# Reordering the attention steps on each engine, and a convolution accumulator and feature sums that use PSUM

## The chip, the core and the metric

One core of a Trainium2 chip runs the whole program. Its engines are TensorE (matmuls; PE in the profile, with the weight loads in a row of their own, PEld), VectorE (DVE), ScalarE (ACT), GpSimd (POOL) and SyncE (SP), which here only issues DMAs. Each engine takes its instructions in the order in which they were written into its queue; semaphores hold one back until what it needs is done. The metric is the device time of one execution in microseconds (us), the median of three runs.

## The reference, cut to what matters

Three stages follow each other on 8 batches of 576 positions (8 heads of 64):

```python
def _attn_ref(q, k, v, w_phi):            # linear attention
    def phi(x):
        proj = x @ w_phi                  # 64 -> 128
        proj = proj - max(abs(proj), axis=-1)
        return concat([exp(proj), exp(-proj)])
    kv = phi(k).T @ v ; z = sum(phi(k))
    return (phi(q) @ kv) / (phi(q) @ z + 1e-6)

def _moe_ref(x, w_val, conv_w, w_out):    # the mixing, d_model 512
    gate = sigmoid(causal_conv(x, conv_w))            # 5 taps per channel
    return (gate * (x @ w_val)) @ w_out

def _moe2_ref(x, w_ch1, w_ch2):           # Fourier mixing, norm, MLP
    u = x + real(fft(fft(x, axis=1), axis=2))
    un = (u - mean) / sqrt(var + 1e-6)
    return u + relu(un @ w_ch1) @ w_ch2
```

The weights of the last two stages arrive as 64-bit floats.

## The kernel before

**Attention.** A pair of batches and a pair of heads make a unit; there are 16 units, each cut into 5 groups of position chunks (four groups of two chunks and one of a single chunk), so TOT = 80 pieces. `run_attention` is a loop over steps `st`, written in a manual schedule: the order of the calls in a step is the order on every engine. A piece passes through these calls, each some steps after the first:

- `emit_P` (step 0): TensorE projects keys and queries into the PSUM tile `pj` (two buffers).
- `emit_Y` (1): VectorE takes the maximum (L210) and subtracts it (L211) into `y`, which frees `pj`.
- `emit_kE` (1): ScalarE, two exponentials of the key half (L219, L220).
- `emit_KV` (2): TensorE, keys by values into `kv`; `emit_kvT` (2): VectorE copies `kv` out (L253).
- `emit_yT` (2): TensorE transposes the query half of `y` into a `tr` buffer (L261), and ScalarE takes two exponentials out of it, `qe` (L263, L264). There are two `tr` buffers, used in turn by `emit_yT` and `emit_XT`.
- `emit_num` (5): TensorE, queries by `kv` into `nm` (one buffer, L279); `emit_X` (5): VectorE divides (L288 to L290), which frees `nm`; `emit_XT` (6): TensorE transposes the quotient (L303), ScalarE copies it to `xT` (L307), SP stores it to `x_scr`.

Between these the weights are converted from 64 bits: 21 generators (`convert`), each resumed at four steps (`lead`): a load from SP, then VectorE L94 and ScalarE L95, then L97, L98 and GpSimd L99 and L100, then ScalarE L102 (the sign) and GpSimd L103 and L104. For the first four of them `done` adds a ScalarE copy (L66) that needs the result of L104. Steps 72 on load the first two batches of the mixing (`load_x`, into the two buffers which the raw weights used too).

**Mixing.** `emit_taps` makes the convolution of one channel block in an SBUF tile `acc` (two buffers): ScalarE writes the first tap (L412), VectorE adds four (L414, scalar_tensor_tensor, read and written in place). `emit_V` takes its sigmoid (L426), multiplies it into the product `val` from PSUM (L434), and makes sums (`gs`) and their high and low parts (`ge`, ScalarE and GpSimd). `emit_W` multiplies by w_out into PSUM tiles `x2p`, copies them out on ScalarE (L457) and, for c of 2 and 3, makes the sums and differences `fs` of two SBUF operands on VectorE (L462), whose high and low parts `fh` feed the transform along features (`emit_FD`, tiles `yp`); `emit_SD` does the one along positions (`abp`). `x2p`, `yp` and `abp` take turns in one PSUM pool of six banks; `val` has two. `split_x` makes the high and low parts `xh` of the next batch on ScalarE and GpSimd. The order here is not written out: the framework's list scheduler sets it from a timing model of its own. The convolutions of the first two blocks (batch 0, m of 0 and 1) are issued in the attention's last steps, each as a whole, in steps 78 and 80, and `emit_V(0, m)` in steps 81 to 84.

**The rest.** The last batch pair (`run_last`) and the MLP (`run_mlp`) are ordered by a planner (`place_ops`) and are not touched but for the pool that two of six PSUM tiles of `run_last` come from.

## Time and profile before

| | us |
|---|---|
| median of three runs | 1487.26 |
| the three runs | 1485.99 to 1487.38 |
| the profiled execution | 1487.67 |
| its span, first to last instruction | 1485.9 |
| TensorE busy | 1358.8 |
| VectorE busy | 1286.4 |
| ScalarE busy | 813.6 |
| GpSimd busy | 743.5 |

The time outside the span is 1.8 us. Times in the trace count from the start of the span. The attention loop takes the first 340 us, its last steps and the first products of the mixing reach to about 395, the mixing to about 655, `run_last` to about 730, the MLP to the end.

### The profile page before, as it was taken

Reading aid. Unit: us, or ns where it says so; the run is one execution under the profiler, and the core shown is the slowest. Engines: PE = TensorE matmul, PEld = TensorE weight load, DVE = VectorE, ACT = ScalarE, POOL = GpSimd, SP = SyncE. Lnnn points to the kernel's source line nnn. Section 1 sums busy time; section 2 is a strip of 40 time slices with the busy share of each in tenths; the row PEclk is TensorE's granted clock in tenths of the full one; section 3 lists DMA queues with packets and bytes.
Section 4 is the critical chain, followed back from the end, with each engine's and each line's share of the span. In section 5 each row is a group of like instructions: output and inputs, shape, how many; then the busy total and the mean of one; then the engine's idle time right before and its main releaser. Section 6 shows DMA issues by size and latency. Waiting matters only on the chain.

```text
span 1485.9 us, 35178 instructions
## 1 busy us (share of the span) xinstructions
PE 1358.8 (91%) x14672; PEld 1305.0 (88%) x14672; DVE 1286.4 (87%) x1938; ACT 813.6 (55%) x1513; POOL 743.5 (50%) x526
## 2 busy tenths in 40 slices
PE   5899999898799999996889999999999999999998
PEld 5788888787788898896789999999999999999998
DVE  5688888877999999989899999999989878887776
ACT  4777787764444444454645555555556544454442
POOL 3847777732577878846455655555526111111111
PEclk8899999999899999997899999999999999999999
DMA  6347766661133333233542223232233222222211
GB/s 218 134 157 269 256 236 245 237 226 40 63 121 128 135 135 104 96 131 126 173 139 92 89 77 114 86 114 94 90 119 105 85 83 86 86 86 86 79 43 51
DMA packets 89852, 186.99 MB, mean 126 GB/s; under 512 B 10455, under 2 KB 37335, under 8 KB 87518
## 3 DMA queue, kind: packets, MB, share of 16 engines
q1 hardware_dynamic: 88488, 181.33, 35.8%
q10 hardware_dynamic: 1206, 3.41, 0.6%
q8 instruction: 115, 1.88, 0.5%
q14 instruction: 43, 0.35, 0.1%
HBM read 121.79 MB, written 62.93 MB: 124 GB/s over the span
## 4 chain that ended last, share of the span: by engine, by line
PE 36%; DVE 28%; POOL 13%; issue 8%; ACT 7%; DMA 6%; SPq 0%; DVEq 0%; POOLq 0%; ACTq 0%
PE cx L857 9%; PE x L788 9%; PE cy L857 5%; PE y L788 4%; DVE acc L414 3%; DVE A L629 3%; DMA raw<-in_w_ch_dram 3%; DVE c L629 3%; PE z L788 3%; DVE acc L629 2%; PE cz L857 2%; POOL ge L75 2%; DVE s L733 2%; POOL mt L100 2%; POOL xh L75 2%
## 5 line engine op out<-in xcount | busy, mean ns | idle before, releaser
L857 PE MATMUL cx<-h,w 128*128 128x256 f32 x1152 | 175.4, 285 | 4.8 <-ACT h L66 2.5
L857 PEld LDWEIGHTS cx<-h,w 128*128 128x128 f32 x1152 | 157.5, 193 | 6.7 <-ACT h L66 3.1
L414 DVE SCALAR_TENSOR_TENSOR acc<-xf,cw,acc 128x576 f32<-128x576 f32 x128 | 137.4, 1078 | 9.1 <-ACT acc L412 7.5
L629 POOL TENSOR_TENSOR c<-c,c 128x512 f32<-128x512 f32 x35 | 49.8, 1424 | 167.6 <-ACT h L632 127.9
L66 ACT ACTIVATE h<-c 128x512 fp32r<-128x512 f32 x180 | 111.7, 627 | 39.8 <-DVE c L629 22.4
L629 DVE TENSOR_TENSOR acc<-cx,acc 128x512 f32<-128x512 f32 x144 | 98.1, 681 | 33.8 <-PE cx L857 33.0
L788 PE MATMUL x<-un,w 128*128 128x256 f32 x864 | 117.2, 286 | 6.7 <-DVE eo L629 6.0
L75 POOL TENSOR_TENSOR h<-c,h 128x512 fp32r<-128x512 f32 x33 | 48.3, 1465 | 149.6 <-ACT h L66 149.3
L632 ACT ACTIVATE c<-c 128x512 f32<-128x512 f32 x108 | 67.9, 630 | 99.8 <-DVE c L629 98.5
L857 PE MATMUL cy<-h,w 128*128 128x256 f32 x864 | 117.3, 285 | 5.2 <-ACT un L66 2.3
L788 PEld LDWEIGHTS x<-un,w 128*128 128x128 f32 x864 | 109.9, 193 | 7.6 <-issue 6.2
L857 PEld LDWEIGHTS cy<-h,w 128*128 128x128 f32 x864 | 108.9, 192 | 7.7 <-DVE h L72 2.5
L72 DVE TENSOR_TENSOR h<-c,h 128x512 fp32r<-128x512 f32 x111 | 104.4, 941 | 1.2 <-ACT h L66 0.5
L240 PE MATMUL kv<-vraw,ke 128*64 128x66 f32 x2560 | 97.5, 231 | 8.4 <-DVE kvT L253 4.9
L203 PE MATMUL pj<-wp,kqraw 64*128 64x128 f32 x1152 | 91.7, 298 | 14.4 <-DMA kqraw<-in_k_dram 7.1
L240 PEld LDWEIGHTS kv<-vraw,ke 128*64 128x64 f32 x2560 | 85.6, 143 | 19.4 <-DVE kvT L253 5.1
L203 PEld LDWEIGHTS pj<-wp,kqraw 64*128 64x128 f32 x1152 | 75.5, 198 | 29.3 <-issue 13.1
L99 POOL TENSOR_SCALAR mt<-mt 128x1024 f32<-128x1024 f32 (+1 forms) x21 | 55.7, 2650 | 88.3 <-DVE r L288 52.7
L211 DVE TENSOR_TENSOR y<-pj,m 128x1024 f32<-128x1024 f32 (+1 forms) x80 | 89.5, 1118 | 8.7 <-ACT xT L307 0.5
L210 DVE TENSOR_REDUCE m<-pj 128x8 f32<-128x1024 f32 (+1 forms) x80 | 88.6, 1108 | 5.5 <-PE pj L203 5.5
L75 POOL TENSOR_TENSOR ge<-gs,ge 128x580 fp32r<-128x580 f32 x32 | 53.6, 1675 | 76.8 <-ACT ge L66 76.8
L79 PE MATMUL val<-xh,wv 128*128 128x288 f32 x256 | 77.3, 307 | 11.2 <-DVE gv L434 11.2
(249 smaller groups left out, 4284.2 us busy)
## 6 DMA issues: line engine op xcount, KB each, us to landing
raw<-in_w_ch_dram SPq DMA_DIRECT2D x16, 1024.0 KB, 7.4
wr<-w_scr SPq DMA_DIRECT2D x32, 448.0 KB, 3.6
vraw<-in_v_dram SPq DMA_DIRECT2D x16, 660.0 KB, 7.7
x_scr<-xT SPq DMA_DIRECT2D x32, 288.0 KB, 5.1
xf<-x_scr SPq DMA_DIRECT2D x8, 1152.0 KB, 5.9
out_dram<-acc SPq DMA_DIRECT2D x36, 256.0 KB, 2.2
kqraw<-in_k_dram SPq DMA_DIRECT2D x15, 576.0 KB, 6.8
kqraw<-in_q_dram SPq DMA_DIRECT2D x15, 576.0 KB, 7.0
```

The source lines that it names most:

```text
L66: nc.scalar.activation(out=dst, in_=src, func=ACTF.Copy)
L72: nc.vector.tensor_tensor(out=dst, in0=src, in1=f32(hi), op=ALU.subtract)
L75: nc.gpsimd.tensor_tensor(out=dst, in0=src, in1=f32(hi), op=ALU.subtract)
L79: mm(o, ah, bh, start=first, stop=False)
L203: mm(p[:, h, o:o + F], t[r, w, 128 * c:128 * c + 128], wp[r, :], start=True, stop=True)
L210: nc.vector.tensor_reduce(out=m, in_=pv, axis=AX.X, op=ALU.max, apply_absolute_value=True)
L211: nc.vector.tensor_tensor(out=y, in0=pv, in1=m.unsqueeze(3).to_broadcast([128, 2, 2 * n, F]), op=ALU.subtract)
L240: mm(t[p, w, :], e[:, a, h, j, p], tv[:, h, slot, :], start=slot % 5 == 0 and w == 0, stop=slot % 5 == 4 and w == 3, skip_group_check=True)
L414: nc.vector.scalar_tensor_tensor(out=acc, in0=x[:, m, t:t + S], scalar=cw[:, m, t:t + 1], in1=acc, op0=ALU.mult, op1=ALU.add)
L629: op(e, cols, lambda e: (nc.vector if e == "v" else nc.gpsimd).tensor_tensor(out=o, in0=x, in1=y, op=alu), r, w)
L788: mm(p[:, n], l, v[:, kt], start=first and n + kt + m == 0, stop=kt == 1 and m == 2, skip_group_check=True)
L857: mm(p[:, o], v, r[:, n], start=first and o + n + m == 0, stop=n + m == 3, skip_group_check=True)
```

## The change

In `run_attention`, a step now issues `emit_X`, `emit_yT` and `emit_XT` first (each of X and XT one step later than before, so that their place behind the previous step's calls is the same), then `emit_P`, `emit_Y`, the weight pieces, `emit_kE`, `emit_KV`, `emit_kvT`, and `emit_num` last. The last resumption of a weight piece comes two steps after the third instead of one. The pools of `e` and `y` lose a buffer each; `xs` gains one. The convolutions of the first two blocks are split over steps 73 to 80, one VectorE tap each, and `emit_V(0, m)` is issued in steps 81, 82, 84 and 86.

In the mixing, from block 2 of batch 0 on, `acc` is a PSUM tile (one buffer, two banks, half of the positions in each), which ScalarE writes and VectorE updates there; the sigmoid goes from it to an SBUF tile `sg`. The sums `fs` take one operand straight from the PSUM tile of the product, each as soon as its product is there. The common pool of PSUM banks shrinks from six to four; `run_last` gets its other two from a pool that is opened when the mixing's are closed.

```diff
--- before.py
+++ after.py
@@ -150,15 +150,16 @@
     P["xf"] = pool(gx, "xf", 2, side=R)
     P["xh"] = pool(gx, "xh", 1, side=R)
     P["g"] = pool(gx, "g", 2, side=R)
-    e_p = pool(early, "e", 4, side=R)
-    y_p = pool(early, "y", 3, side=R)
+    e_p = pool(early, "e", 3, side=R)
+    y_p = pool(early, "y", 2, side=R)
     stg = pool(early, "stg", 2, side=R)
     vraw_p = pool(early, "vraw", 2, side=R)
     ps_pj = pool(early, "ps_pj", 2, PSUM, side=R)
     ap1 = pool(att, "ap1", 1)
     qe_p = pool(att, "qe", 4)
     sm_p = pool(att, "sm", 2)
-    xs_p = pool(att, "xs", 2)
+    xs_p = pool(att, "xs", 3)
+    xT_p = pool(att, "xT", 2)
     ps_tr = pool(att, "ps_tr", 2, PSUM)
     ps_kv = pool(att, "ps_kv", 1, PSUM)
     ps_nm = pool(att, "ps_nm", 1, PSUM)
@@ -302,7 +303,7 @@
         for j in range(n):
             nc.tensor.transpose(t[:, j, :], x[:, j].rearrange("p h d -> p (h d)"), ident)
         if g == 0:
-            xT[u] = xs_p.tile([128, 2 * S], F32, tag="xT", name="xT")
+            xT[u] = xT_p.tile([128, 2 * S], F32, tag="xT", name="xT")
         o = xT[u][:, 128 * cs[0]:128 * (cs[0] + n)]
         nc.scalar.activation(out=o, in_=t.rearrange("p c s -> p (c s)"), func=ACTF.Copy)
         if g == NG - 1:
@@ -368,11 +369,12 @@
         P["g0"] = pool(gx, "g0", 1, side=R)
         P["ws"] = pool(vx, "ws", 2, side=R)
         P["psv"] = pool(vx, "psv", 2, PSUM, side=R)
+        P["psa"] = pool(vx, "psa", 1, PSUM, side=R)
 
     def open_mix2():
         P["x2"] = pool(mx, "x2", 1)
         P["fs"] = pool(mx, "fs", 1)
-        P["ps"] = pool(mx, "ps", 6, PSUM)
+        P["ps"] = pool(mx, "ps", 4, PSUM)
         one = pool(mx, "one", 1)
         P["xr"] = [one.tile([128, NE], F32R, name=f"xr{i}") for i in range(2)]
         P["rem"] = [one.tile([128, NL], F32R, name=f"rem{a}") for a in range(2)]
@@ -406,15 +408,27 @@
 
     taps = {}
 
-    def emit_taps(b, m):
+    def tap_steps(b, m):
         x = xf[b]
-        acc = P["g"].tile([128, S], F32, tag="acc", name="acc")
-        nc.scalar.activation(out=acc, in_=x[:, m, 4:4 + S], func=ACTF.Copy, scale=cw[:, m, 4:5])
+        if "psa" in P:
+            acc = P["psa"].tile([128, 2, 512], F32, tag="pa", name="acc")[:, :, 0:HS]
+        else:
+            acc = P["g"].tile([128, 2, HS], F32, tag="acc", name="acc")
+
+        def shifted(t):
+            return x[:, m, t:t + S].rearrange("p (a s) -> p a s", a=2)
+        nc.scalar.activation(out=acc, in_=shifted(4), func=ACTF.Copy, scale=cw[:, m, 4:5])
         for t in range(4):
             nc.vector.scalar_tensor_tensor(
-                out=acc, in0=x[:, m, t:t + S], scalar=cw[:, m, t:t + 1], in1=acc, op0=ALU.mult, op1=ALU.add
+                out=acc, in0=shifted(t), scalar=cw[:, m, t:t + 1], in1=acc, op0=ALU.mult, op1=ALU.add
             )
+            if t < 3:
+                yield
         taps[b, m] = acc
+        yield
+
+    def emit_taps(b, m):
+        drain(tap_steps(b, m))
 
     def emit_V(b, m):
         h, l = xhl[b]
@@ -422,8 +436,9 @@
             geo[b] = tuple(P[f"g{b % 2}"].tile([128, 4, 2, NE], F32R, tag=f"g{i}", name="ge") for i in range(2))
         if (b, m) not in taps:
             emit_taps(b, m)
-        acc = taps.pop((b, m))
-        nc.scalar.activation(out=acc, in_=acc, func=ACTF.Sigmoid)
+        t = taps.pop((b, m))
+        acc = P["g"].tile([128, S], F32, tag="sg", name="sg")
+        nc.scalar.activation(out=acc.rearrange("p (a s) -> p a s", a=2), in_=t, func=ACTF.Sigmoid)
         gv = P["g"].tile([128, S + 2], F32, tag="gv", name="gv")
         for n in range(2):
             p = P["psv"].tile([128, HS], F32, tag="ps", name="val")
@@ -455,11 +470,12 @@
                 ws = slice(c * 128, (c + 1) * 128)
                 mm3(p, (wo[0][:, kk, ws], wo[1][:, kk, ws]), (gh[:, kk, a], gl[:, kk, a]), kk == 0, kk == 3)
             nc.scalar.activation(out=t[:, c, a, :], in_=p, func=ACTF.Copy)
+            if c >= 2:
+                if a == 0:
+                    fs = P["fs"].tile([128, 2, NE], F32, tag="fs", name="fs")
+                nc.vector.tensor_tensor(out=fs[:, a], in0=t[:, c - 2, a], in1=p, op=(ALU.add, ALU.subtract)[a])
         if c >= 2:
             c0 = c - 2
-            fs = P["fs"].tile([128, 2, NE], F32, tag="fs", name="fs")
-            for a, op in ((0, ALU.add), (1, ALU.subtract)):
-                nc.vector.tensor_tensor(out=fs[:, a], in0=t[:, c0, a], in1=t[:, c, a], op=op)
             fh, fl = fhl[b]
             hi_act(fh[:, c0], fs)
             lo_dve(fl[:, c0], fs, fh[:, c0])
@@ -981,7 +997,8 @@
             o_act(u[0:1, 2], w[96:97], ACTF.Copy, S, wk + [("u", 0, 0), ("u", 0, 1)], [("u", 0, 0), ("u", 0, 1)])
         o_dma([(u_scr[b].rearrange("c p s -> p c s"), u)], [("u", i, j) for i in range(2) for j in range(2)], [("u_scr", b)], 1152, K["su"])
     def run_last(b):
-        ps = [P["ps"].tile([128, 512], F32, tag="ps", name=f"ps{i}") for i in range(6)]
+        ps = [P["ps"].tile([128, 512], F32, tag="ps", name=f"ps{i}") for i in range(4)]
+        ps += [P["ps2"].tile([128, 512], F32, tag="ps2", name=f"ps{i}") for i in (4, 5)]
         ring = ((("ps", i % 6), ps[i % 6]) for i in range(1000))
         tl["fs"] = P["fs"].tile([128, 2, NE], F32, tag="fs", name="fs")
         tl["eo"] = P["x2"].tile([128, 2, 4, NE], F32, tag="eo", name="eo")
@@ -1140,39 +1157,43 @@
 
 
     def run_attention():
-        lead = (0, 3, 4, 5)
+        lead = (0, 3, 4, 6)
         todo = {}
+        tap0 = chain(tap_steps(0, 0), tap_steps(0, 1))
+        taps_at = range(X_AT + 1, X_AT + 9)
         for i in range(len(pieces)):
             for l in lead:
                 todo.setdefault(i * (X_AT - 2 - lead[-1]) // (len(pieces) - 1) + l, []).append(pieces[i])
         n_t = 2 * len(tables)
         did_t = 0
         with tc.manual_schedule():
-            for st in range(TOT + 7):
+            for st in range(TOT + 8):
                 u, g = divmod(st, NG)
 
                 def at(lag):
                     return 0 <= st - lag < TOT
 
+                if at(6):
+                    emit_X(st - 6)
+                if at(2):
+                    emit_yT(st - 2)
+                if at(7):
+                    emit_XT(st - 7)
                 if at(0):
                     emit_P(st)
                 if at(1):
                     emit_Y(st - 1)
+                for c in todo.get(st, ()):
+                    next(c)
+                if at(1):
                     emit_kE(st - 1)
                 if at(2):
                     emit_KV(st - 2)
+                    emit_kvT(st - 2)
+                if st in taps_at:
+                    next(tap0)
                 if at(5):
                     emit_num(st - 5)
-                if at(2):
-                    emit_kvT(st - 2)
-                for c in todo.get(st, ()):
-                    next(c)
-                if at(2):
-                    emit_yT(st - 2)
-                if at(5):
-                    emit_X(st - 5)
-                if at(6):
-                    emit_XT(st - 6)
                 if g == 1 and u >= 1 and u + 1 < NU:
                     load_kq(u + 1)
                 if g == 2 and u >= 1 and u + 1 < NU:
@@ -1186,13 +1207,11 @@
                     load_x(1)
                 if 0 <= st - X_AT - 2 < 4:
                     split_x(0, (st - X_AT - 2,))
-                if st in (TOT - 2, TOT):
-                    emit_taps(0, (st - TOT + 2) // 2)
                 if st == TOT + 1:
                     early.close()
                     open_mix()
-                if 1 <= st - TOT < 5:
-                    emit_V(0, st - TOT - 1)
+                if st - TOT in (1, 2, 4, 6):
+                    emit_V(0, (1, 2, 4, 6).index(st - TOT))
 
 
     if True:
@@ -1228,6 +1247,7 @@
             vx.close()
             gx.close()
             P["x2b"] = pool(mx, "x2b", 1)
+            P["ps2"] = pool(mx, "ps2", 2, PSUM)
             open_mlp()
             run_last(b)
             break
```

## Rows read from the trace of the kernel before

**Rows 1.** The page: busy time and share of the span of each engine.

```profile
PE 1358.8 (91%) x14672; PEld 1305.0 (88%) x14672; DVE 1286.4 (87%) x1938; ACT 813.6 (55%) x1513; POOL 743.5 (50%) x526
```

**Rows 2.** Busy time of each engine in four stretches (us from the span's start): length, then PE, PEld, DVE, ACT and POOL busy, the granted TensorE clock, the DMA engines' share and GB/s.

```profile
20.00:340.00 320.00, 284.86 (x6009) 253.14 (x6007) 257.94 (x446) 239.49 (x456) 216.72 (x94) 0.98 0.60 211
340.00:395.00 55.00, 38.38 (x456) 36.40 (x453) 44.21 (x76) 23.87 (x44) 15.27 (x15) 0.81 0.16 54
395.00:655.00 260.00, 239.85 (x1746) 233.22 (x1745) 247.90 (x382) 119.18 (x264) 197.71 (x192) 0.98 0.33 114
730.00:1486.00 756.00, 726.02 (x5963) 716.99 (x5962) 663.76 (x930) 383.67 (x661) 277.93 (x202) 1.00 0.28 90
```

**Rows 3.** Who waited for whom in the attention loop (0 to 345 us): total us, times, longest.

```profile
PE yt L261 <- ACT qe L264: 16.8, 13, 4.4
...
ACT cv L102 <- POOL mt L100: 16.1, 16, 1.9
...
ACT wv L66 <- POOL mt L104: 7.0, 2, 4.0
...
PE xt L303 <- ACT qe L264: 5.5, 1, 5.5
```

**Rows 4.** Timeline (start, us, engine, line, operation) of ScalarE, GpSimd and TensorE at the end of one of the first four weight pieces; in brackets the idle time before and what ended it.

```profile
59.52 1.16 ACT L102 ACTIVATE cv<-raw 128x1024 f32<-128x1024 int32 x1
63.87 1.06 ACT L66 ACTIVATE wo<-mt 128x1024 fp32r<-128x1024 f32 x1 [3.19 <-POOL mt L104]
...
61.50 2.34 POOL L104 TENSOR_TENSOR mt<-mt,cv 128x1024 f32<-128x1024 f32 x1
...
65.95 1.10 PE L261 MATMUL yt<-ident,y 128*128 128x128 f32 x4 [4.35 <-ACT qe L264]
```

**Rows 5.** Timeline of VectorE and TensorE: the end of `emit_Y` against the start of the transposes `yt` of the piece before, in the first and the last of 20 steps (of 73 looked at, steps 7 to 79) in which the transposes started first.

```profile
73.62 1.23 DVE L211 TENSOR_TENSOR y<-pj,m 128x1024 f32<-128x1024 f32 x1
...
74.77 0.44 PE L261 MATMUL yt<-ident,y 128*128 128x128 f32 x2
...
334.15 1.23 DVE L211 TENSOR_TENSOR y<-pj,m 128x1024 f32<-128x1024 f32 x1
...
334.97 0.66 PE L261 MATMUL yt<-ident,y 128*128 128x128 f32 x4
```

**Rows 6.** Timeline of VectorE, SP and ScalarE around the load of the mixing's first two batches (step 72) and its first use.

```profile
316.55 0.07 DVE L395 MEMSET xf<- 128x16 f32 x1
...
319.62 0.16 DVE L288 TENSOR_SCALAR r<-nm 128x4 f32<-128x4 f32 x1 [1.66 <-PE nm L279]
...
318.71 0.95 SPq L396 DMA_DIRECT2D xf<-x_scr  x2
...
328.29 0.68 ACT L66 ACTIVATE xh<-xf 128x576 fp32r<-128x576 f32 x1 [3.38 <-DMA xf<-x_scr]
```

**Rows 7.** Timeline of VectorE, TensorE and ScalarE between the attention and the mixing.

```profile
341.58 3.38 DVE L414 SCALAR_TENSOR_TENSOR acc<-xf,cw,acc 128x576 f32<-128x576 f32 x4 [1.75 <-ACT acc L412]
...
347.75 2.91 PE L240 MATMUL kv<-vraw,ke 128*64 128x66 f32 x48 [4.87 <-DVE kvT L253]
...
375.25 10.84 DVE L414 SCALAR_TENSOR_TENSOR acc<-xf,cw,acc 128x576 f32<-128x576 f32 x8 [0.94 <-ACT acc L412]
...
384.23 0.68 ACT L426 ACTIVATE acc<-acc 128x576 f32<-128x576 f32 x1 [4.49 <-DVE acc L414]
...
386.52 0.61 PE L79 MATMUL val<-xh,wv 128*128 128x288 f32 x1 [9.06 <-DVE gv L434]
```

**Rows 8.** What TensorE waited for in the mixing (395 to 655 us): total us, times, longest.

```profile
PE yp L79 <- ACT fh L66: 10.7, 6, 2.6
PE val L80 <- POOL xh L75: 8.2, 14, 2.7
```

**Rows 9.** Busy time in one iteration of the mixing loop, columns as in rows 2.

```profile
457.66:496.65 38.99, 35.47 (x262) 34.37 (x262) 37.75 (x59) 18.14 (x41) 31.28 (x30) 1.00 0.37 129
```

**Rows 10.** Durations of the operations that the change touches or is priced by. The first two and the last rows are groups (busy us, mean ns | idle before); in the others a number like 790/870/1903 is least/median/most ns. First four iterations (435 to 592 us), then three of them, the whole mixing, and the MLP.

```profile
L414 DVE SCALAR_TENSOR_TENSOR acc<-xf,cw,acc 128x576 f32<-128x576 f32 x64 | 68.5, 1071 | 2.2 <-ACT acc L412 1.5
...
L462 DVE TENSOR_TENSOR fs<-x 128x290 f32<-128x290 f32 x16 | 18.2, 1136 | 0.0
...
L414 DVE SCALAR_TENSOR_TENSOR acc<-xf,cw,acc x48: 790/870/1903, 460.6 to 573.0; 128x576 f32<-128x576 f32 x48
...
L434 DVE TENSOR_TENSOR gv<-val,acc x24: 440/446/451, 458.3 to 574.5; 128x288 f32<-128x288 f32 x24
...
L75 POOL TENSOR_TENSOR xh<-xf,xh x24: 1408/1932/1965, 418.1 to 623.1; 128x576 fp32r<-128x576 f32 x24
...
L832 DVE SCALAR_TENSOR_TENSOR h<-x,h 128x512 fp32r<-128x512 f32 x35 | 24.0, 685 | 0.6
```

**Rows 11.** Timeline of ScalarE, VectorE and TensorE between the last product of `emit_W` and the transform along features, in the iteration of rows 9.

```profile
489.29 0.30 PE L81 MATMUL x2p<-ge,wo 128*128 128x290 f32 x1
...
491.67 1.70 DVE L462 TENSOR_TENSOR fs<-x 128x290 f32<-128x290 f32 x1
...
495.17 0.70 DVE L462 TENSOR_TENSOR fs<-x 128x290 f32<-128x290 f32 x1
...
495.91 0.69 ACT L66 ACTIVATE fh<-fs 128x580 fp32r<-128x580 f32 x1
...
496.65 0.39 PE L79 MATMUL yp<-ft,fh 128*128 128x258 f32 x1 [1.95 <-ACT fh L66]
```

## Prediction

> **What bounds the kernel now.** The page's first part, read first, shows two engines near their limit, TensorE and VectorE [rows 1], so the time has to be looked at by stage. The table of stretches comes next [rows 2]. In the attention loop TensorE is busy 285 of 320 us and VectorE 258, and neither is full. In the 55 us behind it TensorE idles 17 us, at a mean granted clock of 0.81. In the mixing VectorE is busy 248 of 260 us and TensorE 240. In the MLP TensorE is busy 726 of 756 us, and the change does not touch it. What can be won lies before 730 us, and it is TensorE's idle time there: about 35, 17 and 20 us in the three stretches, since TensorE's work stays the same.
>
> The list of waits says what ended that idle time. In the attention loop 22.3 us (16.8 and 5.5) ended with an exponential `qe`, because a transpose had no free `tr` buffer [rows 3]. Such a stall has this shape [rows 4]: ScalarE stands at the copy of a converted weight until GpSimd's L104 is done, the `qe` exponentials are queued behind it, and TensorE's `yt` waits 4.35 us. Smaller ones come from the sign L102, which waits 16.1 us in all for GpSimd's L100 [rows 3]. In the mixing TensorE waited 10.7 us for `fh` and 8.2 us for `xh` [rows 8], with VectorE busy 37.75 of 38.99 us of an iteration [rows 9].
>
> **Mixing, VectorE.** An iteration has 16 tap operations at a mean of 1.071 us and four `fs` at 1.136 us: 17.1 + 4.5 = 21.7 us [rows 10]. The taps without disturbance take 0.790 us, and some 1.903 us; `gv`, with as many operands but one of them in PSUM, stays within 0.440 and 0.451 us over 24 instances [rows 10]. The difference is GpSimd, whose `xh` runs between 1.408 and 1.965 us at the same time: two engines that lose time together when both VectorE operands lie in SBUF. [...]
>
> With one operand in PSUM, `fs` is priced as `gv` plus two columns, 0.45 us. For a tap, the nearest row is L832, the same operation with a PSUM input at 512 columns, 0.685 us [rows 10]. With the slope between 288 and 512 columns, (0.685 - 0.446)/224 = 1.07 ns a column, 576 columns take 0.75 us. No row shows VectorE or ScalarE writing PSUM; the bounds for a tap are 0.75 and 1.90 us, the most that a tap took here, and I take 0.85 us, near the rows. So VectorE's iteration falls from 37.75 to 37.75 - 21.7 + 16 x 0.85 + 4 x 0.45 = 31.5 us, and it stops being the limit. [...]
>
> **Mixing, TensorE.** It then bounds the iteration: its 35.5 busy us [rows 9]. The `fh` wait shows how. The last `x2p` ended at 489.6; its two `fs` started 2.1 and 5.6 us later, behind taps and in contention; `fh` followed and TensorE resumed at 496.65 [rows 11]. Read straight from PSUM, the second `fs` needs neither ScalarE's copy nor a long queue: about 489.6 + 1.0 to its end, + 0.7 for `fh`, about 492, before TensorE reaches the transform. `xh` comes 0.5 us sooner for each of four chunks, if GpSimd is undisturbed (1.408 against 1.932 us at the median). What is late next is the PSUM ring: with four banks in place of six, and a bank held until `fs` has read it, fewer transform products can start early. Of the 18.9 us of waits [rows 8] I take 17 us as gained. Bounds: 0 (each wait comes back as one for a bank) and 20 us.
>
> **Attention steps.** Cyclically, TensorE's order changes in one thing: the transposes of a piece run one step sooner, before `emit_P` in place of behind `emit_num`. ScalarE's weight pieces move in front of `kE`, and VectorE's in front of `kvT`. SP's and GpSimd's order between the parts stays, but the last resumption of a piece, with its store, comes a step later, when L99 to L103 are done. The sign then waits for nothing, and the copy behind it waits for L104 alone, 2.3 us [rows 4]. So a block of ScalarE that was 59.5 to 64.9 in rows 4 (sign and copy with the waits) shrinks by a microsecond or two, and `qe` stands ahead of it. Of the 22.3 us I take 14 as gained; bounds 5 (only the smaller stalls go) and 22.
>
> Against it stand three things. First, a transpose needs the `y` of its piece, and now one step sooner, right where the previous piece's transposes stand today. In 20 of 73 steps that `y` was not finished then, from 0.08 us (74.85 against 74.77) to 0.41 in the last of them (335.38 against 334.97) [rows 5], and up to 1.7 us. `emit_P`, 0.8 us later, has to wait for the same `y` today, so at most 0.8 us a step is new: 8.0 us over the 20. I take 6, bounds 0 and 9. The pool of two `y` costs nothing by itself, since its transposes are a whole step ahead.
>
> Second, the first tap is now in step 73, one step behind the load that feeds it. VectorE's clearing of the tile, the last thing of step 72, is at 316.55, the load is issued at 318.71, and ScalarE's first use had to wait for it until 328.29 [rows 6]. In step 73 ScalarE's first tap and VectorE's behind it stand there from about 319 to 329; queued behind them is the next `emit_X`, which ran at 319.62 [rows 6] and frees `nm`, and behind that `emit_Y`. TensorE can go on for about a step. I take 9 us of loss, bounds 3 (as ScalarE's wait now) and 10. Third, in return, the four taps in one piece go, behind which `kvT` was late and TensorE idle 4.87 us [rows 7]: 5 us gained; one tap a step fits beside VectorE's waits for `nm`. The attention steps sum to -14 + 6 + 9 - 5 = -4 us.
>
> **Between the two.** TensorE idles 9.06 us for a `gv` while VectorE works through eight taps of two blocks in turn, 10.84 us, 1.36 each, before the first block's sigmoid at 384.23 [rows 7]. With one PSUM accumulator the second chain can't start before that sigmoid, so the first one takes 4 x 0.85 = 3.4 us and the sigmoid comes near 379.5. Then `xh` and `ge` of GpSimd are late next. I take 5 us gained, bounds 0 and 8. The spread of `emit_V` over steps 81 to 86, the `xs` and `xT` pools and `run_last`'s other banks I cost at nothing: their work is unchanged, and TensorE has its own work beside them; without that cover a step of the tail is about 2 us.
>
> **Sum.** -17 - 4 - 5 = -26 us, against the profiled execution: 1487.7 - 26 = 1461.7. The median of the runs is 0.4 us below that execution, so 1461 us.
>
> **Rivals.**
> - The attention loop loses: only 5 us of stalls go, the `y` wait costs 8, the load 10, the taps return 5: +8 in place of -4, 1473 us. For it speaks that VectorE and TensorE run in lock step there [rows 5]; against it, the size of the stalls by weight pieces.
> - The PSUM ring takes most of the mixing's gain: transform products that run early today find no bank until a late `fs` has read it, and the 1.95 us of [rows 11] stay in each of six iterations: 12 us, so -5 in place of -17, 1473 us. Against it: `fs` itself comes earlier. Both together: near 1485.
> - The other side: updating the accumulator in PSUM is dear. VectorE's iteration is 17.9 + 16p us for a tap of p us. At 0.97 busy, as now, it meets today's 39 us at p = 1.24, and with the other 9 us gained the kernel is slower by 3 from p = 1.37. At p = 1.9 the iteration is 49.8 us, 65 us more in six: about 1543. L832 speaks against it, but reads PSUM only.
> - More: every stall by the weight pieces goes and the `y` wait is absorbed: -19 in the attention, 1446 us.
> - If a tap with one operand in PSUM still loses time to GpSimd, taps stay at 1.07 us and the iteration at 35 us of VectorE work: most of the 17 would still come, so this is inside the forecast's range.
>
> **How the numbers follow.** Forecast 0.50, with its own range 1451 to 1470; more 0.09; attention 0.15; ring 0.11; both 0.07; dear PSUM 0.08. A change under 0.2% (3 us) can't be told from none here. Faster: 0.50 + 0.09 + 0.15 + 0.11 and 0.01 of both = 0.86; within 0.2%: 0.05 of both; slower: 0.08 + 0.01 = 0.09. The range reaches from a little below "more" to the edge of "both": 1443 to 1481.
>
> **What would show it.** Taps of 0.75 to 0.9 us with little spread, `fs` at 0.45, VectorE some 32 us busy in an iteration of 35.5 to 36.5, and nearly no TensorE wait for `fh`. In the attention loop, no `yt` behind `qe` of over 2 us, but waits of `yt` for `y`, and a gap of VectorE of about 9 us at step 73. The forecast is wrong if taps exceed 1.2 us, if TensorE waits for `x2p` or `yp` banks by more than 1 us an iteration, or if the loop's 320 us don't shrink.

## The result, and the profile after

The median is 1452.7 us (1450.1 to 1454.9), against 1487.2 before: a ratio of 0.9766 (0.9749 to 0.9784), by which it is 34.8 us faster. The forecast was 1461 us, 26 less than before. The profiled execution has a span of 1453.0 us, 32.9 less. Where they went is read from marks: starts of the same instructions in each trace (the subtraction of `emit_Y` for some pieces, and the first and last product `x2p`), in us from the span's start. The experiments of the next section are included; each ratio is to runs of before taken beside that kernel.

| kernel | piece 70 | piece 73 | piece 79 | first x2p | last x2p | span | ratio to before (95%) |
|---|---|---|---|---|---|---|---|
| before | 310.86 | 321.69 | 349.60 | 391.48 | 646.65 | 1485.9 | |
| after | 303.95 | 321.06 | 346.44 | 379.36 | 615.02 | 1453.0 | 0.9766 (0.9749 to 0.9784) |
| mixing alone | 311.29 | 322.12 | 350.13 | 386.48 | 623.96 | 1459.5 | 0.9819 (0.9795 to 0.9843) |
| accumulator alone | 310.99 | 321.82 | 350.32 | 384.94 | 626.13 | 1463.0 | 0.9813 (0.9791 to 0.9836) |
| sums alone | 309.69 | 320.52 | 349.14 | 390.13 | 643.12 | 1480.8 | 0.9974 (0.9954 to 0.9993) |
| ring of four alone | 309.91 | 320.74 | 349.69 | 391.33 | 655.10 | 1492.5 | 1.0062 (1.0035 to 1.0088) |
| attention alone | 303.29 | 320.06 | 346.71 | 377.29 | 646.41 | 1482.6 | 0.9985 (0.9968 to 1.0002) |
| late resumption alone | 305.50 | 316.33 | 343.75 | 385.18 | 641.13 | 1479.2 | 0.9949 (0.9931 to 0.9967) |
| after, transposes put back | 300.63 | 318.39 | 344.29 | 377.95 | 614.14 | 1451.7 | 0.9754 (0.9734 to 0.9774) |
| after, `emit_V` close | 302.54 | 319.35 | 345.90 | 381.51 | 617.27 | 1454.1 | 0.9800 (0.9776 to 0.9825) |
| after, taps from step 75 | 303.51 | 314.87 | 341.80 | 372.44 | 608.75 | 1446.1 | 0.9726 (0.9706 to 0.9746) |
| after, late copy | 293.54 | 310.20 | 337.43 | 368.83 | 604.46 | 1442.8 | 0.9698 (0.9676 to 0.9720) |
| after, both of these | 293.64 | 305.00 | 331.94 | 363.37 | 599.59 | 1436.8 | 0.9668 (0.9650 to 0.9687) |
| both, transposes put back | 294.38 | 305.20 | 332.59 | 365.52 | 601.75 | 1439.6 | 0.9660 (0.9641 to 0.9680) |

From before to after, piece 79 is 3.2 us earlier (346.44 against 349.60), the way from there to the first `x2p` is 9.0 shorter (32.92 against 41.88), the mixing between first and last `x2p` 19.5 shorter (235.66 against 255.17), and the rest 1.3. The forecast had 4, 5, 17 and 0. The stretches between the marks don't hold quite the same work, though: in after, 24 products `val` have moved from ahead of the first `x2p` to behind it, and 42 products of the last pieces from behind the start of piece 79 to ahead of it. The rows of the two middle stretches (columns as in [rows 2]), in before and then in after, part the gain:

```profile
349.60:391.48 41.88, 30.13 (x336) 28.57 (x332) 33.09 (x57) 18.03 (x31) 13.68 (x9) 0.80 0.19 63
391.48:646.65 255.17, 236.21 (x1719) 230.01 (x1718) 245.11 (x377) 116.54 (x254) 195.84 (x190) 0.98 0.33 115
...
346.44:379.36 32.92, 25.18 (x271) 23.51 (x267) 16.24 (x40) 10.40 (x19) 4.29 (x3) 0.84 0.08 30
379.36:615.02 235.66, 231.44 (x1744) 228.58 (x1742) 212.32 (x391) 121.70 (x264) 169.10 (x195) 1.00 0.37 130
```

Of the 9.0 us, 4.0 are idle time of TensorE and 5.0 its busy time; of the 19.5, 14.7 are idle time and 4.8 busy time.

The busy times of after (as in [rows 1]), its first two stretches, and one iteration of its mixing loop (columns as in [rows 2, 9]):

```profile
PE 1346.5 (93%) x14672; PEld 1296.5 (89%) x14672; DVE 1246.7 (86%) x1938; ACT 813.5 (56%) x1513; POOL 710.2 (49%) x526
...
20.00:340.00 320.00, 282.28 (x5999) 251.66 (x5995) 268.08 (x448) 240.78 (x458) 220.61 (x99) 0.98 0.60 211
340.00:395.00 55.00, 46.13 (x519) 43.66 (x518) 36.40 (x74) 23.26 (x47) 14.01 (x11) 0.91 0.16 54
...
474.66:509.41 34.75, 34.62 (x264) 34.24 (x262) 31.39 (x59) 18.08 (x41) 25.64 (x30) 1.00 0.40 145
```

The iteration took 38.99 us with VectorE 37.75 busy [rows 9]. It now takes 34.75, VectorE has work for 31.39 (the forecast worked out 31.5), and TensorE is busy for all but 0.13 us. TensorE's idle time in the 55 us behind the attention fell from 17 to 9 us, and the mean granted clock there rose from 0.81 to 0.91 [rows 2]; but the last 15.6 us of that stretch are mixing in after, and 3.5 in before. In the loop's row hardly anything changed for TensorE: it idles 38 of the 320 us. Over the whole execution TensorE's busy time fell by 12.3 us (1358.8 to 1346.5) with the same 14672 products, so idle time makes only 20.6 of the 32.9. The mean granted clock rose from 0.972 to 0.982; how much of the 12.3 us that is isn't told apart, since in the two iterations the clock is 1.00 and the busy time fell too (35.47 to 34.62).

Durations in after (least/median/most ns), which answer to [rows 10] (8 of the 128 taps, those of the first two blocks, still have their accumulator in SBUF):

```profile
L420 ACT ACTIVATE acc<-xf,cw x32: 729/749/774, 317.5 to 612.7; 128x576 f32<-128x576 f32 x32
L422 DVE SCALAR_TENSOR_TENSOR acc<-xf,cw,acc x128: 800/815/824, 318.3 to 616.9; 128x576 f32<-128x576 f32 x128
L441 ACT ACTIVATE sg<-acc x32: 627/652/687, 351.4 to 617.8; 128x576 f32<-128x576 f32 x32
L476 DVE TENSOR_TENSOR fs<-x,x2p x28: 439/449/457, 392.1 to 617.7; 128x290 f32<-128x290 f32 x28
L75 POOL TENSOR_TENSOR xh<-xf,xh x32: 1406/1432/1668, 324.2 to 589.4; 128x576 fp32r<-128x576 f32 x32
```

The tap, 790 to 1903 ns before, has lost its spread. By the trace of before, 85 of the 120 taps from block 2 of batch 0 on ran while GpSimd was at an instruction, and took 802 to 2085 ns; the other 35 took 789 to 819. In after 88 ran beside GpSimd, and took 800 to 824. And `fs` costs what `gv` cost (449 ns against 446 at the median), and GpSimd's `xh` has come down from a median of 1932 ns to 1432.

What TensorE (first three rows) and ScalarE (next three) waited for in the attention loop of after, 20 to 340 us, and what TensorE waited for in its mixing, 379 to 618 us (next two), and behind the loop, 340 to 395 us (last three):

```profile
PE yt L262 <- DVE y L212: 13.3, 24, 1.3
PE kv L241 <- ACT ke L220: 9.8, 4, 4.3
PE nm L280 <- DVE xs L291: 6.6, 3, 4.7
...
ACT wv L66 <- POOL mt L104: 6.6, 2, 4.0
ACT wo L66 <- POOL mt L104: 5.7, 2, 3.1
...
ACT cv L102 <- POOL mt L100: 1.8, 3, 0.6
...
PE val L79 <- DVE gv L449: 2.0, 2, 1.5
PE val L80 <- POOL xh L75: 1.7, 2, 0.9
...
PE nm L280 <- DVE xs L291: 4.6, 3, 2.1
PE xt L304 <- DVE xs L291: 2.2, 1, 2.2
PE yt L262 <- DVE y L212: 1.6, 2, 0.9
```

In the mixing no `fh`, no bank and almost no `xh` is waited for any more [rows 8]. In the attention the wait of `yt` for `qe` is gone, and so is most of the sign's wait for L100 [rows 3]. But new names stand there with as much time in all: the transposes wait for `y`, and four products `kv` wait for `ke`. These four are the stalls of [rows 4], with another instruction behind the same copy. Timeline of after, ScalarE, GpSimd and TensorE, at the end of the same weight piece:

```profile
59.11 1.20 ACT L102 ACTIVATE cv<-raw 128x1024 f32<-128x1024 int32 x1
63.42 1.06 ACT L66 ACTIVATE wo<-mt 128x1024 fp32r<-128x1024 f32 x1 [3.12 <-POOL mt L104]
...
60.69 2.71 POOL L104 TENSOR_TENSOR mt<-mt,cv 128x1024 f32<-128x1024 f32 x1
...
66.06 0.34 PE L241 MATMUL kv<-vraw,ke 128*64 128x66 f32 x4 [3.39 <-ACT ke L220]
```

And step 73 of after (SP, ScalarE, VectorE, TensorE), with the tap behind its load:

```profile
307.25 1.28 SPq L398 DMA_DIRECT2D xf<-x_scr  x2
...
317.53 0.77 ACT L420 ACTIVATE acc<-xf,cw 128x576 f32<-128x576 f32 x1 [5.40 <-DMA xf<-x_scr]
...
318.33 0.82 DVE L422 SCALAR_TENSOR_TENSOR acc<-xf,cw,acc 128x576 f32<-128x576 f32 x1 [7.23 <-ACT acc L420]
...
320.04 2.00 PE L280 MATMUL nm<-kvT,qe 128*64 128x65 f32 x32 [4.67 <-DVE xs L291]
```

The load is issued 10.3 us before its data is used; ScalarE, VectorE and, a step later, TensorE stand still for it. Piece 72 is 6.9 us ahead of before (310.41 against 317.27) and piece 73 only 0.6.

### The profile page after: what moved, and what is told of

It is laid out like the page before. It is cut to its first block, busy times and chain, and to the rows that moved or that the text cites. A ratio compares the mean times of both kernels' runs of the same rounds, so it can differ in the third digit from the quotient of the medians.

```text
span 1453.0 us, 35130 instructions
## 1 busy us (share of the span) xinstructions
PE 1346.5 (93%) x14672; PEld 1296.5 (89%) x14672; DVE 1246.7 (86%) x1938; ACT 813.5 (56%) x1513; POOL 710.2 (49%) x526
## 4 chain that ended last, share of the span: by engine, by line
PE 42%; DVE 31%; POOL 11%; issue 10%; ACT 4%; DMA 2%; DVEq 0%; POOLq 0%; SPq 0%; ACTq 0%
PE cx L873 9%; PE x L804 9%; PE cy L873 5%; PE y L804 4%; DVE A L645 3%; DVE c L645 3%; DVE m L211 3%; DVE y L212 3%; PE z L804 3%; PE kv L241 2%; DVE acc L645 2%; PE cz L873 2%; PE nm L280 2%; DVE s L749 2%; PE pj L204 2%
## 5 line engine op out<-in xcount | busy, mean ns | idle before, releaser
L422 DVE SCALAR_TENSOR_TENSOR acc<-xf,cw,acc 128x576 f32<-128x576 f32 x128 | 104.2, 814 | 12.5 <-ACT acc L420 11.3
L280 PE MATMUL nm<-kvT,qe 128*64 128x65 f32 x2304 | 85.7, 228 | 14.0 <-DVE xs L291 11.2
L75 POOL TENSOR_TENSOR ge<-gs,ge 128x580 fp32r<-128x580 f32 x32 | 46.5, 1453 | 95.4 <-ACT ge L66 90.5
L204 PE MATMUL pj<-wp,kqraw 64*128 64x128 f32 x1152 | 88.3, 292 | 4.5 <-DMA kqraw<-in_k_dram 4.5
L280 PEld LDWEIGHTS nm<-kvT,qe 128*64 128x64 f32 x2304 | 78.3, 143 | 15.4 <-issue 14.4
```

Source lines behind the costliest of these rows:

```text
L75: nc.gpsimd.tensor_tensor(out=dst, in0=src, in1=f32(hi), op=ALU.subtract)
L204: mm(p[:, h, o:o + F], t[r, w, 128 * c:128 * c + 128], wp[r, :], start=True, stop=True)
L280: mm(t[p, 2 * j + h, 0:65], e[:, a, h, j, p], kt[:, 2 * h + a, b, :], start=(a == 0), stop=(a == 1))
L422: nc.vector.scalar_tensor_tensor(out=acc, in0=shifted(t), scalar=cw[:, m, t:t + 1], in1=acc, op0=ALU.mult, op1=ALU.add)
```

## Experiments

The theory: the accumulator in PSUM takes VectorE's taps and GpSimd's additions out of each other's way, and with that VectorE out of the limit; the attention's order gives little, since it moves waits rather than ends them. The main rival: the terms of the forecast simply add up, each from its own edit.

### The parts one by one

**Mixing alone**: after with the old `run_attention`. **Attention alone**: after with the old accumulator, ring and sums (the sigmoid still goes to a tile of its own).

> The changed kernel with the attention loop of before: the same order of steps, taps and lead as before, but the accumulator in PSUM, the ring of four banks and the sums from PSUM. Theory (mixing and attention add up, the accumulator frees both the taps and GpSimd's additions): 17 to 25 us faster than before, about 1463 to 1470; taps 0.81 to 0.83 us, no wait of the triples for fh. Rival (most of the gain comes from the reordering, the accumulator alone saves little): 5 us or less, 1482 or more.

> The attention loop, taps placement and lead of the changed kernel, with the accumulator and the sums of before (SBUF, ring of six). Theory: piece 79 starts about 3 us earlier and the transition, whose normalisation is spread over later stages, saves some more: 4 to 12 us faster, 1475 to 1483. Rival (the attention order loses, the rest hides it): slower than before by up to 8, 1495. Second rival (the bunched taps bring the loss at step 73 with the accumulator in SBUF too): the gain shrinks to 0 to 4.

Alone, the mixing's edits give 26.9 us (1 - 0.9819, of 1487), a little over the 25 expected at most, and the attention's 2.2, an amount that can't be told from none, where 4 to 12 were expected. Together they give 34.8: about 6 more than the sum, which by the three intervals is uncertain by some 5. The marks show it more clearly. With the attention edits alone piece 79 is 2.9 us earlier and the first `x2p` even 14.2, but the last `x2p` only 0.2: the mixing takes 269.12 us in place of 255.17. Part of that is the 24 products that crossed the mark here too. From piece 79 to the last `x2p`, which holds them in every kernel, it is 297.05 us before, 299.70 with the attention alone, 273.83 with the mixing alone and 268.58 in after: with the old accumulator the attention's edits lose 2.7 us on this way, with the new one they gain 5.3. Right behind the start of the mixing the row of the attention run (columns as in [rows 2]) is

```profile
395.00:460.00 65.00, 56.37 (x387) 54.49 (x387) 64.16 (x96) 30.68 (x62) 50.46 (x49) 0.88 0.34 118
```

VectorE is busy 64.16 of 65 us. It bounds this kernel, and when the first `x2p` starts it has done only 17 of its taps, against 23 in before, so that the products that start earlier wait longer. After has done even fewer by then (15), but VectorE is busy for only 57.50 us there, and the lead stays to the end. So the terms don't add: a gain ahead of a stretch counts only where the engine that bounds the stretch gains it too. The second rival of the attention run, that VectorE's taps at step 73 bring their stall with the old accumulator too, holds as well: 7.5 us of lead at piece 72 (309.76 against 317.27), 1.6 at piece 73.

**Accumulator alone, sums alone, ring alone.** The first is the mixing run without this; the second is before with this alone:

```diff
+            if c >= 2:
+                if a == 0:
+                    fs = P["fs"].tile([128, 2, NE], F32, tag="fs", name="fs")
+                nc.vector.tensor_tensor(out=fs[:, a], in0=t[:, c - 2, a], in1=p, op=(ALU.add, ALU.subtract)[a])
...
-            fs = P["fs"].tile([128, 2, NE], F32, tag="fs", name="fs")
-            for a, op in ((0, ALU.add), (1, ALU.subtract)):
-                nc.vector.tensor_tensor(out=fs[:, a], in0=t[:, c0, a], in1=t[:, c, a], op=op)
```

and the third is before with the following (and, as in after, with two of `run_last`'s tiles from a pool of their own):

```diff
-        P["ps"] = pool(mx, "ps", 6, PSUM)
+        P["ps"] = pool(mx, "ps", 4, PSUM)
```

> The kernel before with the accumulator in PSUM and the ring of four that it needs; the sums x + x2p read two SBUF operands as before, and the attention loop is that of before. Theory (the accumulator carries the mixing's gain, because it takes VectorE's taps out of the contention and VectorE out of the limit): taps 0.81 to 0.83 us, sums 0.6 to 1.1, 14 to 23 us faster than before, 1465 to 1474. Rival (both edits are needed, since the waits for fh end with the sums): under 10 us, 1478 or more, with more than 1.5 us an iteration waited for fh.

> The kernel before with only the sums x + x2p read from PSUM; accumulator in SBUF, ring of six, order of before. Theory (the taps and GpSimd's additions hold each other up on the shared SBUF path, and the sums have only a small part in it): taps stay at 1.0 us or more, 0 to 8 us faster, 1479 to 1487. Rival (the earlier release of fs is what removes the triples' wait, and carries the mixing's gain): 12 us or more, 1475 or less.

> The kernel before with only the ring of matmul banks cut from six to four in the mixing. Theory (no bank is waited for): within 3 us of before. Rival (a ring of four holds the projections up when evictions are late): 1 to 2 us an iteration, 5 to 15 slower, 1492 to 1502.

The accumulator alone (with the ring of four) gives 27.8 us, by the ratios as much as with the sums (by the marks, the last `x2p` comes 2.2 us earlier with them: 623.96 against 626.13), and more than the theory's upper 23. The sums alone give 3.9, inside the 0 to 8 expected. Groups of the mixing (395 to 620 us) with the accumulator alone, then with the sums alone (busy us, mean ns | idle before):

```profile
L422 DVE SCALAR_TENSOR_TENSOR acc<-xf,cw,acc 128x576 f32<-128x576 f32 x104 | 84.5, 813 | 7.8 <-ACT acc L420 7.2
...
L453 DVE TENSOR_TENSOR gs<-gv 128x290 f32<-128x290 f32 x50 | 34.5, 729 | 0.3
...
L477 DVE TENSOR_TENSOR fs<-x 128x290 f32<-128x290 f32 x25 | 15.2, 607 | 1.6 <-ACT x L472 1.5
```

```profile
L414 DVE SCALAR_TENSOR_TENSOR acc<-xf,cw,acc 128x576 f32<-128x576 f32 x94 | 110.4, 1174 | 3.0 <-ACT acc L412 1.9
...
L461 DVE TENSOR_TENSOR fs<-x,x2p 128x290 f32<-128x290 f32 x24 | 10.7, 445 | 0.7 <-ACT x L457 0.7
```

With the taps in PSUM the sums `fs` with two SBUF operands fall from 1136 ns [rows 10] (1068 over this stretch) to 607. This need not be the accumulator's doing: with the ring alone they fall to 633, and `gs`, with two SBUF operands as well, rises from 599 ns in before to 729 with the accumulator alone. In before 27 of the 28 `fs` ran beside a GpSimd instruction, at 1085 ns in the mean, and the other took 449; of the 64 `gs` 24 did, at 757, and the other 40 took 453 in the mean. How many met it in the two other kernels was not counted. With the sums alone the taps still meet GpSimd, at 1174 ns. What TensorE waited for in that kernel's mixing: the wait for `fh` falls from 10.7 to 3.0 us, and that for `xh` rises from 8.2 to 12.5 [rows 8]:

```profile
PE val L80 <- POOL xh L75: 12.5, 15, 3.0
PE yp L79 <- ACT fh L66: 3.0, 6, 0.6
```

The ring alone was a surprise: 9.2 us slower, where I expected nothing. Busy time in its mixing, the groups of its taps and its `fs` (395 to 620 us), and what TensorE waited for:

```profile
395.00:655.00 260.00, 235.98 (x1691) 228.47 (x1691) 253.25 (x367) 115.45 (x251) 192.15 (x190) 0.97 0.32 113
```

```profile
L414 DVE SCALAR_TENSOR_TENSOR acc<-xf,cw,acc 128x576 f32<-128x576 f32 x90 | 112.5, 1250 | 0.9
...
L462 DVE TENSOR_TENSOR fs<-x 128x290 f32<-128x290 f32 x23 | 14.6, 633 | 0.6 <-ACT x L457 0.4
```

```profile
PE yp L79 <- ACT fh L66: 18.6, 6, 3.9
PE val L80 <- POOL xh L75: 4.9, 8, 1.6
```

Still no bank is waited for, so the rival's cause is not there, though its size is. With four banks the list scheduler sets another order on VectorE too, and the taps take 1250 ns in the mean, where before has 1084 over the same stretch. They meet GpSimd more: of the 120 taps from block 2 on, 90 run beside a GpSimd instruction in place of 85, and these take 1392 ns in the mean in place of 1214. VectorE is busy 253 of 260 us, and the wait for `fh` grows from 10.7 to 18.6. That the order is the cause is argued from these facts, not tried. In the kernel after, where the taps beside GpSimd lose no time (814 ns in the mean, the others 817), nothing of it is left to see.

### The attention's steps

**Late resumption alone**: before with `lead = (0, 3, 4, 6)` in place of `(0, 3, 4, 5)` (some weight pieces also start a step sooner by it, as in after).

> The kernel before with only the last resumption of a weight piece one step later. Theory (the sign's and the copy's waits for GpSimd make the stalls of the transposes behind qe, and a step more removes them): piece 70 starts 4 to 7 us earlier; as VectorE bounds the stretch behind the loop, the end gains 0 to 4, 1483 to 1487. Rival (the place of the weight pieces before the exponentials of the keys is what removes them): piece 70 moves by less than 2 us.

Piece 70 comes 5.4 us earlier, where 4 to 7 were expected, and the whole of it arrives at the end: 7.6 us by the ratio, 6.7 by the span, beyond the 4 that I allowed. Here VectorE's own work comes earlier too, so the mixing starts and ends 6 us sooner, unlike in the attention run (the first tap of block 2 starts 6.2 us earlier than in before, there 1.7). ScalarE's 16.1 us of waits of the sign [rows 3] are gone from the list, but in TensorE's list that of `yt` behind `qe` remains, and is even larger:

```profile
PE yt L261 <- ACT qe L264: 19.6, 13, 4.5
```

The four long ones among these, by the copies of the first weight pieces, are all still there, and at piece 20 this kernel is 2.3 us behind before (104.53 against 102.22). What it gains comes behind that, where nearly all of the sign's waits lay. So the theory holds for the sign's waits and fails for the copy's.

**Transposes put back**: after with `emit_yT(st - 2)` behind `emit_num` again, as in before.

> The changed kernel with the query transposes put back behind the numerators, so that TensorE's sequence is that of before; weight pieces, lead, taps and mixing stay changed. Theory (the stalls behind qe went with the weight pieces' new place, and the earlier transposes only added waits for y, 13 us in 24 places, of which the projection behind would have waited for the rest anyway): 3 to 8 us faster than the changed kernel, 1445 to 1450, no wait of yt behind qe over 2 us. Rival (the earlier transposes are what gives ScalarE the time): the stalls behind qe return with 5 us or more, 1455 to 1465.

0.9754 against 0.9766: no difference, where 3 to 8 us were expected. The waits of `yt` for `y` went (13.3 us), and piece 70 came 3.3 us earlier, piece 79 2.2, the last `x2p` 0.9. What came in their place, in TensorE's list (20 to 340 us):

```profile
PE kv L241 <- ACT ke L220: 12.3, 8, 5.0
PE nm L280 <- DVE xs L291: 6.7, 2, 5.6
PE nm L280 <- issue: 3.5, 4, 1.5
PE pj L204 <- DVE y L212: 3.1, 7, 0.7
```

Neither case is right in full: no wait of `yt` behind `qe` came back, so the weight pieces' new place had removed them, with the late resumption (which by itself left them), and not the earlier transposes; but the waits for `y` were nearly free.

**Taps from step 75**: after with

```diff
-        taps_at = range(X_AT + 1, X_AT + 9)
+        taps_at = (X_AT + 3, X_AT + 4, X_AT + 5, X_AT + 6, X_AT + 6, X_AT + 7, X_AT + 7, X_AT + 8)
```

(and as many taps in a step as it stands there).

> The changed kernel with the taps of the first two blocks in steps 75 to 80, so that the load they read has landed. Theory (the first tap in step 73 waits for the load and holds the whole loop up by 6.3 us): piece 79 starts 5 to 7 us earlier, 1445 to 1448. Rival (the taps, two to a step now, hold kvT up instead and give it back): piece 79 moves by less than 2 us, 1451 to 1454.

Piece 73 comes 6.2 us earlier than in after and the last `x2p` 6.3; piece 79 4.6 (5 to 7 were expected), probably since two taps in a step cost a little. By the ratios it is 0.0040 of 1487, or 6 us. The first tap's wait, in VectorE's timeline, is now

```profile
321.51 0.82 DVE L422 SCALAR_TENSOR_TENSOR acc<-xf,cw,acc 128x576 f32<-128x576 f32 x1 [1.88 <-ACT acc L420]
```

**Late copy**: after with the end of a weight piece one step behind its last products.

```diff
         nc.gpsimd.tensor_tensor(out=w, in0=w, in1=sg, op=ALU.mult)
+        yield
         done(w.rearrange("p (k f) -> p k f", k=shape[0]))
...
-        lead = (0, 3, 4, 6)
+        lead = (0, 3, 4, 6, 7)
```

(the pieces start as in after, so the last one ends a step later).

> The changed kernel with the copy (or store) that ends a weight piece one step behind the sign and the last two products, so that ScalarE's copy of the first four pieces finds L104 done. Theory (the four waits of that copy, 12.3 us on ScalarE, are what holds the exponentials of the keys up, 9.8 us of TensorE's waits): these waits end, piece 50 starts 5 to 10 us earlier, and the end comes 5 to 10 us earlier, 1443 to 1448. Rival (VectorE or the waits for y take the time back): less than 2 us, 1451 to 1455.

It is 10 us faster than after (0.9698 against 0.9766), a little over the theory's range, and piece 20 already comes 7.0 us earlier (93.50 against 100.50). In the list of waits (20 to 340 us) the products behind `ke` and ScalarE's copies have

```profile
PE kv L242 <- ACT ke L221: 4.0, 5, 1.2
...
ACT wo L66 <- POOL mt L104: 1.9, 2, 1.4
...
ACT wv L66 <- POOL mt L104: 0.7, 1, 0.7
```

That is 4.0 us in place of 9.8, and 2.6 in place of 12.3. The stall of [rows 4] was there all the time, in both kernels. The other 3.4 us by which piece 70 is ahead of after (293.54 against 303.95) come behind piece 20, and these rows don't say from where.

**Both of these**, and both with the transposes put back:

> The changed kernel with both: the taps of the first two blocks in steps 75 to 80, and the copy that ends a weight piece one step later. Theory (two separate stalls, which add up): 9 to 15 us faster than the changed kernel, 1438 to 1444. Rival (VectorE's own pace in the loop bounds it): no better than the later taps alone, 1447 to 1450.

> The kernel with both later taps and later copies, and with the query transposes put back behind the numerators. In the kernel with both, transposes wait 18.3 us in 26 places for y of the same step. Theory (the projection behind would wait for that same y, so these waits cost little): within 2 us of the kernel with both, 1436 to 1440. Rival (they cost what the list of waits shows): 6 us or more faster, 1432 or less. On the other side (the transposes behind the numerators meet the exponentials qe late): 3 us or more slower, 1441 or more, with waits of yt for qe.

Both together: 1438.4 us (1437.9 to 1438.6), 0.9668 of before and 14.6 us less than after (0.0098 of 1487): the two stalls add up, and this kernel beats both. The list of waits shows 18.3 us of `yt` behind `y` in it. Putting the transposes back takes them off the list and gives 1437.7 (1437.1 to 1441.7), ratio 0.9660 (0.9641 to 0.9680): nothing. (The profiled execution, whose marks the table has, is the slowest of its five.) The line of the kernel with both, and two of those with the transposes put back (20 to 340 us):

```profile
PE yt L263 <- DVE y L213: 18.3, 26, 1.6
...
PE kv L242 <- ACT ke L221: 6.0, 11, 1.1
PE pj L205 <- DVE y L213: 5.0, 10, 0.8
```

The projection `pj` now waits for `y` as the theory said, but only for 5.0 us; the rest of what came back is spread over other waits.

**`emit_V` close**: after with `emit_V(0, m)` in steps 81, 82, 83 and 84.

> The changed kernel with emit_V(0, m) in steps 81, 82, 83 and 84 as before in place of 81, 82, 84 and 86. Theory (the spread is what made the transition gain 9 us in place of the 5 forecast, since with the accumulator alone it gained 5): TensorE waits for gv again, 3 to 4 us, and the first x2p starts 3 to 5 us later, 1455 to 1458. Rival (the spread costs and gives nothing; the taps' place gives the rest): within 1.5 us of the changed kernel.

From piece 79 to the first `x2p` it takes 35.61 us, 2.7 more than after and 6.3 less than before. So the spread is worth 2.7 us there, less than the theory's 3 to 5 (and 2.3 at the last `x2p`), and TensorE's wait for `gv` did not return as expected; `xh` is waited for instead (4.8 us). The end is 1.1 us later by the span, 5 by the ratios.

## Why the prediction came out as it did

- **Mixing, VectorE: right.** Its iteration was worked out as 31.5 us and measures 31.39; a tap was put at 0.85 us and takes 0.815, `fs` at 0.45 and takes 0.449. These prices hold only if neither loses time to GpSimd any more. No row of before shows that for a tap or for `fs`; it was my estimate from `gv` alone (51 of its 64 instances in before ran beside GpSimd, at 440 to 456 ns). The runs showed it: beside GpSimd the taps take 800 to 824 ns with the accumulator in PSUM and took 802 to 2085 with both operands in SBUF, 21 of the 28 `fs` ran beside it, at 439 to 457, and `xh` came down to 1432 ns. They also show that the 16 taps do it and the four `fs` add little (nothing by the ratios, 2.2 us by the marks): of the two edits that I priced together, one carries the term.
- **Mixing, TensorE: a term a little small.** 17 us forecast, 19.5 measured. The term was meant as idle time, and of that 14.7 us went. The rest is TensorE's busy time, which "stays the same" by the prediction (35.47 us an iteration [rows 9]) and came out at 34.62 with as many matmuls in the kernel. The iteration of 34.75 us is thus even below the 35.5 to 36.5 that were named as a sign. No wait for banks came. In the run without the attention's edits, where no products crossed the mark, the same stretch gained 17.7.
- **Between the two: the term held, the spread was left out.** 5 us forecast, 9.0 measured, of which 4.0 are idle time. The accumulator and its sooner sigmoid account for 5.5 (mixing alone: 36.35 us from piece 79 to the first `x2p`, against 41.88, with the same products between), as I had it; the spread of `emit_V`, which I costed at nothing, for 2.7. What is left, under a microsecond, isn't told apart. These shares depend on the order of the edits: the attention's alone shorten this way by 11.3 us (30.58), of which 7.6 are TensorE's busy time, moved to either side.
- **Attention: the sum was near, its parts were not.** Forecast -4, measured -3.2 at piece 79. The step "of the 22.3 us I take 14 as gained" failed in its mechanism. I let `qe` stand ahead of the copy, and left out that `ke` now stands behind it, so the four stalls by the copies, 13.7 of the 22.3 us, went over to `kv` with 9.8 us; and the late resumption, which I didn't price by itself, gives 5.9 alone. The `y` wait was put at 6 us and is worth 2 to 3 (the pieces came 3.3 and 2.2 us earlier without it). That the two errors nearly cancel is luck: piece 70 is 6.9 us ahead, where -14 + 6 is 8. The 4.87 us behind the bunched taps [rows 7] are gone, with no wait for `kvT` in the list of the 55 us behind the loop, but 6.8 us behind `xs` and 1.6 behind `y` stand in that list instead, and from piece 73 to piece 79 after gains 2.5 us (25.38 against 27.91) of the 5 forecast. The count of 20 steps [rows 5] leaves out a 21st, the step of those taps, where the transposes started 5.1 us before `y` ended (342.22 against 347.37). The load's stall was put at 9 (bounds 3 and 10) and costs 6.2, as its removal shows.
- **Adding up: not examined.** The sum treated the three stretches as independent. They were not: with VectorE still the bound, the attention's edits are worth 2 us; with the accumulator in PSUM, about 8 (0.9819 to 0.9766, uncertain by some 4).
- **Rivals.** The attention loop did not lose: -3.2 us at piece 79, where the rival had +8. That the ring takes the gain back did not happen in after (no bank, no `fh` in the list), though the ring alone costs 9.2 us in the old mixing, by another way than the one I named. A dear tap was excluded by 0.815 us, and one that still loses time to GpSimd by its 800 to 824 ns. "More" had the right place, the stalls of the weight pieces, but the change left those by the copies in; the late copy took most of them.

## What to carry to other kernels

Where two engines slow each other down, as VectorE and GpSimd did here with their operands in SBUF (taps of up to 2085 ns, `xh` of 1932 at the median), try moving one operand of the most frequent operation to PSUM; here the 16 taps alone did it (at most 824 ns), and GpSimd's untouched additions became quicker beside them (`xh` 1432). Before adding up gains of successive stretches, see which engine bounds the later one: a head start of another engine was lost there. A mark between two stages moves with the order of the work, so see what lies on either side of it. When a stalled instruction is moved, look for what then stands behind the cause, and price a wait by what the next instruction on that engine would wait for anyway: 18.3 us of listed waits were worth nothing, and one copy issued a step later was worth 10.

## What the runs showed of the hardware

A VectorE tap that reads and writes its accumulator in PSUM takes 815 ns at the median (800 to 824). One on an accumulator in SBUF takes 806 in before (789 to 819) in the 35 cases in which GpSimd runs nothing beside it: in PSUM it took 9 ns more, and what that saved is the time lost beside GpSimd (there the mean was 1214 ns in before and is 814 in after). ScalarE was quicker with PSUM on one side; with the accumulator in SBUF (the run with the ring alone) the durations are (least/median/most ns)

```profile
L412 ACT ACTIVATE acc<-xf,cw x32: 758/777/790, 340.9 to 647.2; 128x576 f32<-128x576 f32 x32
L426 ACT ACTIVATE acc<-acc x32: 667/684/692, 358.7 to 654.9; 128x576 f32<-128x576 f32 x32
```

against 749 for writing into PSUM and 652 for reading from it (of these 32 each, 30 have the accumulator in PSUM), 28 and 32 ns less (18 and 34 less than the medians of before, 767 and 686).
